# The first pass of a fused attention and gated FFN kernel: one program order on all five queues, the low weight bits cut out on ScalarE, and no float32 copies of two weight matrices

## The chip, the core and the metric

The kernel runs on one core of a Trainium2 chip. The metric is the device time of one execution in microseconds. The engines are named as the profile names them: PE (matrix multiply, with its weight loads as PEld), DVE (VectorE), ACT (ScalarE), POOL (GpSimd) and SP (the queue that issues the DMAs). Each engine works through its own queue strictly in order, and an instruction that waits holds up all that stand behind it on that queue.

## What is computed

Eight batches with eight heads of 576 queries and keys of width 64 go through an attention whose keys and values are first averaged in groups of eight, so that there are 72 of them. The result, 4608 rows of 512, goes through a gated feed-forward layer. The three weight matrices come in float64.

```python
k_p = k.reshape(B, H, Sp, pool, D).mean(axis=3)        # pool = 8, Sp = 72; v likewise
attn = softmax(q @ k_p.T / 8)
x = (attn @ v_p) as 4608 x 512
gate = 1 / (1 + exp(-(x @ w_gate)))                    # 512 x 1536
out = (gate * (x @ w_val)) @ w_out                     # 1536 x 512
```

## The kernel before, in words

**Blocks and passes.** The 4608 rows are cut into 12 blocks of 384 (`BT`). Six passes take two blocks each (side 0 and side 1). A pass has two halves: the chains, which make gate and value for 12 column groups `f` of 128 (kind G and V), and the second product, which sums over the 12 groups into six PSUM banks. Every float32 operand is split into a high and a low half of type fp32r, and a product is the three matmuls high·high, high·low, low·high. A chain of the first two passes (`whole`, L517) is thus 12 matmuls of 128x384, and one step of the second product (`second`, L615) is 18 matmuls of 128x512. From the third pass on a scheme with seven instead of eight products is used; the change doesn't touch it.

**Attention.** For a block `j` and a pair of heads `p` the steps are: sum keys in groups of eight on DVE, scale them into a block-diagonal tile on ACT (`kbd`), scores on PE (`sc`), maximum on DVE, exponentials on ACT, their total on DVE, division on POOL (`pm`), transposes on PE (`tp`), a high half on ACT and a low half on DVE, the product with the values on PE (`av`), and a copy into `xs`. The eight keys beyond 64 go a way of their own (`rest`, `r3`, `vres`). When both pairs of a half are there, `xs` is split into `xo`, the operand of the chains. Blocks 2 and 3, which the second pass needs, are computed during the first pass, blocks 4 and 5 during the second, and so on.

**Conversion.** `converted` (L155) takes a quarter-matrix tile of 128x1024 float64 words. `to_f32` (L112) makes float32 of it in five steps: an ACT instruction on the high words (L116), then on DVE a minimum (L118), a shift (L120), the sign (L122) and the three top bits of the low words (L126). Two ACT copies (L164) and two DVE subtractions (L166) make the halves. 12 such tiles make up the first two matrices. All halves go to DRAM (`keep`), and the float32 tile itself goes there too (`keptw`, L171). In the second pass `sums` (L178) loads that tile again and makes sums of quarters for the later passes (L182 to L184, L97, L98). The third matrix is converted in 12 tiles of 128x512 (`convert_o`, L211) beside the first pass's second product.

**What sets the order.** In the first pass the part `first_blocks` (L797) is written out by hand: blocks 0 and 1, tiles 0 and 1 of both matrices and the first eight chains stand in one list, and PE, DVE, ACT and POOL run it in that order. SP's queue there, and everything after this part (`hidden_first`, L541, then `second`), is put in order by a scheduler, which works from its own estimates. Key and value loads of the later blocks go through four buffers (`rawp`). The values of blocks 0 and 1 are pooled by matmuls in float32 (L926, L936), those of later blocks by DVE sums (L273).

Of the kernel before, what the change touches and what calls it, by code (L numbers as in the profile page):

```python
# [12 lines left out]
F32R = mybir.dt.float32r  # L13
U32 = mybir.dt.uint32
# [4 lines left out]
P = 128  # L19
B, H, S, D = 8, 8, 576, 64  # L20
POOL = 8
# [33 lines left out]
PLACE = {"k0": (0, 0), "k1": (0, 576), "k2": (0, 1152), "k3": (0, 1728), "R0": (0, 2304),  # L55
         "q0": (1, 0), "q1": (1, 384), "q2": (1, 768), "q3": (1, 1152), "V0": (1, 1536), "V1": (1, 2048), "V2": (1, 2560),
         "V3": (2, 0), "U0": (2, 512)}
# [3 lines left out]
def attention_then_ffn(ctx: ExitStack, tc: tile.TileContext, qT, kT, vm, vr, vn, sums8, wgv, wo, const, out, outT):  # L61
# [11 lines left out]
    cst = cpool.tile([P, P + 4], F32, name="cst")  # L73
    nc.sync.dma_start(cst, const)
    ident, mask = cst[:, :P], cst[:, P:]
# [30 lines left out]
    kept_w = {(kind, p): dram.tile([P, 4, HALF], F32, name=f"keptw{kind}{p}") for p in range(NP) for kind in "GVO"}  # L106
# [3 lines left out]
    words, parts, plain, oparts = {}, {}, {}, {}  # L110

    def to_f32(w, lo, hi):  # L112

        u = w.bitcast(U32)

        pinned(nc.scalar.activation(w, hi.bitcast(F32), AF.Abs, scale=2.0 ** -112))  # L116
        yield
        nc.vector.tensor_scalar(out=w, in0=w, scalar1=F64_MAX, scalar2=None, op0=ALU.min)  # L118
        yield
        nc.vector.tensor_scalar(out=u, in0=u, scalar1=3, scalar2=None, op0=ALU.logical_shift_left)  # L120
        yield
        nc.vector.scalar_tensor_tensor(  # L122
            out=u, in0=hi, scalar=0x80000000, in1=u, op0=ALU.bitwise_and, op1=ALU.bitwise_or
        )
        yield
        nc.vector.scalar_tensor_tensor(  # L126
            out=u, in0=lo, scalar=29, in1=u, op0=ALU.logical_shift_right, op1=ALU.bitwise_or
        )
        yield

    def fetch(kind, p):
        raw = big.tile([P, 4 * HALF, 2], U32, name="raw64", tag="big")
        nc.sync.dma_start(raw.rearrange("p n t -> p (n t)"), wgv[p, "GV".index(kind)].bitcast(U32))
        words[kind, p] = raw
# [11 lines left out]
    made = [0]  # L146

    def room_for_parts():

        made[0] += 1  # L150
        if made[0] <= 4 * NP and made[0] % 11 in (8, 9, 10):
            return work.tile([P, 2, 2, HALF], F32R, name="parts_x", tag=f"xo{(3, 6, 7)[made[0] % 11 - 8]}")
        return wpool.tile([P, 2, 2, HALF], F32R, name="parts", tag="parts")

    def converted(kind, p):  # L155
# [4 lines left out]
        w = (big if p else wpool).tile([P, 4, HALF], F32, name="w4", tag="big" if p else "parts")  # L160
        yield from to_f32(w.rearrange("p a n -> p (a n)"), raw[:, :, 0], raw[:, :, 1])
# [940 lines left out]
```

## Time and profile before

| | before |
|---|---|
| median of 3 runs | 1011.4 us (1011.3 to 1013.82) |
| the profiled execution | 1011.91 us |
| its span, first to last instruction | 1010.1 us |
| PE busy | 966.0 us (96%) |
| DVE busy | 674.4 us (67%) |
| ACT busy | 518.1 us (51%) |
| DMA | 267.08 MB, mean 264 GB/s |

The views give microseconds from the start of the span. A line such as `L122 DVE SCALAR_TENSOR_TENSOR w<-raw,w 128x1024 ... x12 | 14.6, 1216 | 0.2` reads: line 122 of the kernel, on DVE, 12 instructions that write `w` from `raw` and `w`, busy 14.6 us in all, 1216 ns each on average, and 0.2 us in which DVE stood idle just before them. A float32 matmul leaves two records; an fp32r matmul leaves one. The records of matmuls that run back to back overlap, so the pace of a dense stretch is read from the start of a group to the start of the next. In a table of stages the numbers behind each engine are its busy time and its records; PEclk is the granted clock of TensorE, 1.00 for full speed.

### The profile page before, as it was taken

What the parts mean: (1) busy time and instruction counts of PE and PEld (TensorE: products, weight loads), DVE (VectorE), ACT (ScalarE), POOL (GpSimd) and SP (SyncE); (2) the same over time, 40 slices, a digit from 0 to 9 for tenths busy, and PEclk for the clock granted to TensorE, in tenths of its full rate; (3) what the DMA queues carried; (4) which work ended last, traced back from release to release, by engine and by line L of the source; (5) the groups of instructions that cost most, each with busy time, mean ns of one, the idle gap of its engine ahead of it and who ended that gap; (6) DMA issues with size and microseconds to landing.
All of it is one profiled execution on the core that took longest, in us unless ns stands there. A gap on an engine that the chain in (4) does not pass through costs nothing.

```text
span 1010.1 us, 15339 instructions
## 1 busy us (share of the span) xinstructions
PE 966.0 (96%) x5448; PEld 918.1 (91%) x5448; DVE 674.4 (67%) x1149; ACT 518.1 (51%) x1034; POOL 47.4 (5%) x67
## 2 busy tenths in 40 slices
PE   5779999989999999999989999999999999999998
PEld 4569999768999988889979999998999999999998
DVE  5858898795666635675877666769566659244474
ACT  4647676554344432564645455656365546233342
POOL 2010000000000000000000000000000000000000
PEclk9979999999999999999999999999999999999999
DMA  9736999887999633899986877877877678867556
GB/s 335 247 119 223 337 368 361 272 274 279 344 322 337 223 132 116 307 376 362 320 289 196 288 258 239 267 261 249 288 270 222 217 247 250 289 233 247 195 188 229
DMA packets 117739, 267.08 MB, mean 264 GB/s; under 512 B 12448, under 2 KB 44448, under 8 KB 116128
## 3 DMA queue, kind: packets, MB, share of 16 engines
q1 hardware_dynamic: 117664, 266.12, 77.7%
q8 instruction: 43, 0.70, 0.3%
q14 instruction: 32, 0.26, 0.1%
HBM read 209.44 MB, written 56.62 MB: 263 GB/s over the span
## 4 chain that ended last, share of the span: by engine, by line
PE 79%; DVE 8%; DMA 7%; ACT 4%; issue 2%; SPq 0%; ACTq 0%; DVEq 0%
PE chain L486 30%; PE chain L526 16%; PE acc L725 15%; PE acc L634 8%; PE sc L330 3%; PE av L339 3%; DMA w<-keptwO 1%; PE tp L418 1%; DVE s L660 1%; PE vp L926 1%; DMA raw_o<-in_wo 1%; DVE hs L690 1%; DMA parts<-keptG1C 1%; DMA out<-o 1%; DMA w<-keptwG 1%
## 5 line engine op out<-in xcount | busy, mean ns | idle before, releaser
L486 PE MATMUL chain<-xo,parts 128*128 128x384 f32 x2016 | 375.7, 340 | 4.7 <-DMA parts<-keptV1A 1.1
L486 PEld LDWEIGHTS chain<-xo,parts 128*128 128x128 f32 x2016 | 349.2, 188 | 9.8 <-ACT sG L492 1.7
L526 PE MATMUL chain<-xo,parts 128*128 128x384 f32 x1008 | 188.2, 341 | 3.4 <-ACT parts L164 3.2
L725 PE MATMUL acc<-hs,oparts 128*128 128x384 f32 x1008 | 184.4, 338 | 2.4 <-DMA oparts<-keptS 1.0
L526 PEld LDWEIGHTS chain<-xo,parts 128*128 128x128 f32 x1008 | 175.7, 189 | 5.4 <-ACT parts L164 3.8
L725 PEld LDWEIGHTS acc<-hs,oparts 128*128 128x128 f32 x1008 | 175.8, 189 | 5.1 <-DVE hs L690 2.2
L634 PE MATMUL acc<-oparts,hs 128*128 128x512 f32 x432 | 104.4, 395 | 4.3 <-ACT hs L626 4.1
L634 PEld LDWEIGHTS acc<-oparts,hs 128*128 128x128 f32 x432 | 79.7, 188 | 21.8 <-ACT hs L626 5.2
L498 DVE TENSOR_TENSOR y<-chain,sG 128x384 f32<-128x384 f32 x72 | 39.6, 553 | 73.1 <-DMA out<-o 26.3
L412 POOL TENSOR_TENSOR pm<-e,rz 128x384 f32<-128x384 f32 x40 | 36.3, 907 | 700.5 <-DVE rz L393 415.0
L498 DVE TENSOR_TENSOR y<-chain,sV 128x384 f32<-128x384 f32 x72 | 39.4, 551 | 41.3 <-PE chain L486 30.2
L504 ACT ACTIVATE gate<-y 128x384 f32<-128x384 f32 x72 | 37.7, 525 | 37.8 <-DVE y L498 37.4
L492 ACT COPY sV<-chain 128x384 f32<-128x384 f32 x72 | 34.2, 475 | 44.3 <-PE chain L486 43.0
L690 DVE TENSOR_TENSOR hs<-h,hs 128x768 fp32r<-128x768 f32 x48 | 46.1, 965 | 15.5 <-ACT hs L689 15.5
L492 ACT COPY sG<-chain 128x384 f32<-128x384 f32 x72 | 34.3, 476 | 41.5 <-PE chain L486 41.3
L689 ACT CAST hs<-h 128x768 fp32r<-128x768 f32 x48 | 40.1, 835 | 24.0 <-PE acc L725 23.0
L689 ACT CAST hs<-s 128x768 fp32r<-128x768 f32 x36 | 29.6, 835 | 31.6 <-PE acc L725 21.5
L330 PE MATMUL sc<-kbd,raw 128*128 128x144 f32 (+1 forms) x256 | 42.5, 297 | 0.0
L507 DVE TENSOR_TENSOR h<-y,gate 128x384 f32<-128x384 f32 x72 | 39.7, 555 | 1.7
L330 PEld LDWEIGHTS sc<-kbd,raw 128*128 128x128 f32 (+1 forms) x256 | 33.6, 177 | 7.4 <-issue 4.5
L690 DVE TENSOR_TENSOR hs<-s,hs 128x768 fp32r<-128x768 f32 x36 | 34.3, 959 | 7.3 <-ACT hs L689 7.0
L422 DVE TENSOR_TENSOR pl<-tp,ph 128x384 fp32r<-128x384 f32 x40 | 22.0, 551 | 21.9 <-ACT ph L421 21.9
(159 smaller groups left out, 1177.1 us busy)
## 6 DMA issues: line engine op xcount, KB each, us to landing
oparts<-keptS SPq DMA_DIRECT2D x48, 512.0 KB, 5.0
oparts<-keptO SPq DMA_DIRECT2D x72, 256.0 KB, 3.7
raw<-in_wgv SPq DMA_DIRECT2D x12, 1024.0 KB, 7.7
raw<-in_qT SPq DMA_DIRECT2D x42, 192.0 KB, 4.3
raw<-in_kT SPq DMA_DIRECT2D x28, 288.0 KB, 5.5
raw<-in_vm SPq DMA_DIRECT2D x24, 256.0 KB, 4.6
raw_o<-in_wo SPq DMA_DIRECT2D x12, 512.0 KB, 5.5
keptO<-oparts SPq DMA_DIRECT2D x12, 512.0 KB, 4.2
```

The lines of the kernel that those rows point to most:

```text
L330: nc.tensor.matmul(sc[lo - i * P:hi - i * P, i], lhsT=q[:, lo:hi], rhs=kbd[slot(b, p)], start=True, stop=True)
L412: nc.gpsimd.tensor_tensor(out=pm, in0=e[:, n, :, :KM], in1=rz[:, n, :, None].broadcast_to([P, 2 * QT, KM]), op=ALU.mult)
L486: nc.tensor.matmul(t, lhsT=w[:, h, a], rhs=x[:, y, c], start=(m in (1, 2, 5) and c == 0 and k == 0), stop=(c == 1 and k == 2), skip_group_ ...
L492: nc.scalar.copy(s, t)
L498: nc.vector.tensor_tensor(out=y, in0=t, in1=seen[kind, {2: 1, 3: 6, 7: 5}[m]], op=ALU.add)
L504: nc.scalar.activation(gates[q[0]][:, q[1]], y, AF.Sigmoid)
L507: nc.vector.tensor_tensor(out=hb[f // 4][:, f % 4, q[0] * BT:(q[0] + 1) * BT], in0=y, in1=gates[q[0]][:, q[1]], op=ALU.mult)
L526: nc.tensor.matmul(t, lhsT=w[:, c // 2, h, a], rhs=x[:, y, c % 2], start=(c == 0 and k == 0), stop=(c == NC - 1 and k == 2),)
L634: nc.tensor.matmul(acc[i], lhsT=hs[:, y, a], rhs=o[:, w], start=(f == 0 and k == 0), stop=(f == NF - 1 and k == 2),)
L689: nc.scalar.copy(hs[:, 0], x)
L690: nc.vector.tensor_tensor(out=hs[:, 1], in0=x, in1=hs[:, 0].bitcast(F32), op=ALU.subtract)
L725: nc.tensor.matmul(acc[name, c], lhsT=w[:, k, h, c * P:(c + 1) * P], rhs=hs[:, y, k], start=(m in (1, 2, 5) and q == 0 and k == 0 and t == ...
```

## The change

**One order.** `first_blocks` and `hidden_first` are gone, and so is the scheduled first `second`. `first_pass` runs a table of some 900 words, from left to right, for all of the first pass: attention of blocks 0 to 3, all 24 conversions, all 48 chains, the second product and the stores. SP's loads and stores are in the table too. The loads named in `FIRST` stand ahead of the table; the second to fourth weight tile are no longer among them. An entry like `G.0.3@6` is the gate chain of block 0, group 3, in PSUM bank b4; `lr`, `lv`, `lk`, `lq` are loads; `rsum`, `vsum`, `keys` are sums on DVE.

**Values of block 1.** They are pooled on DVE from `in_vr` and `in_vm` like those of later blocks; only batch 0 is still pooled by matmuls.

**Low bits.** `to_f32` has the three low bits made by an ACT instruction (a scaled Relu on a 16-bit half of the low word), and the DVE shift is folded into the last of DVE's steps. DVE has three steps then instead of four, ACT two instead of one.

**No float32 copies.** `keptw` for the first two matrices is neither stored nor loaded. In the second pass `base` adds the two halves again: two DVE instructions of 128x512 per tile.

```diff
-FIRST = "k0 q0 k1 q1 k2 q2 k3 q3 U0 W0 V0 V1 V2 V3 R0 W1 W2 W3".split()
+FIRST = "k0 q0 k1 q1 k2 q2 k3 q3 U0 W0 V0 V1 V2 V3 R0".split()
+ORDER = """
+lr.1.1 rsum.1.1 rhi.1.1 lv.1.0 vsum.1.0 vhi.1.0 rlo.1.1 keys.0.0 put.0.0 lr.1.0 sc.0.0@0 rsum.1.0 rhi.1.0 rlo.1.0
+vput.1.0 lk.1.0 keys.1.0 vlo.1.0 put.1.0 lv.1.1 vsum.1.1 keys.0.1 lq.1.0 put.0.1 sc.1.0@1 lk.1.1 max.0.0 keys.1.1
...
-    def to_f32(w, lo, hi):
+    def to_f32(w, raw):
         u = w.bitcast(U32)
+        words = raw.rearrange("p (n t) -> p n t", t=2)
+        lo, hi = words[:, :, 0], words[:, :, 1]
         pinned(nc.scalar.activation(w, hi.bitcast(F32), AF.Abs, scale=2.0 ** -112))
         yield
+        half = raw.bitcast(U16).rearrange("p (n t) -> p n t", t=4)[:, :, 1]
+        nc.scalar.activation(lo, half, AF.Relu, scale=2.0 ** -13, bias=third)
+        yield
         nc.vector.tensor_scalar(out=w, in0=w, scalar1=F64_MAX, scalar2=None, op0=ALU.min)
         yield
-        nc.vector.tensor_scalar(out=u, in0=u, scalar1=3, scalar2=None, op0=ALU.logical_shift_left)
-        yield
-        nc.vector.scalar_tensor_tensor(
-            out=u, in0=hi, scalar=0x80000000, in1=u, op0=ALU.bitwise_and, op1=ALU.bitwise_or
-        )
-        yield
-        nc.vector.scalar_tensor_tensor(
-            out=u, in0=lo, scalar=29, in1=u, op0=ALU.logical_shift_right, op1=ALU.bitwise_or
-        )
+        nc.vector.scalar_tensor_tensor(out=lo, in0=hi, scalar=0x80000000, in1=lo, op0=ALU.bitwise_and, op1=ALU.bitwise_or)
+        yield
+        nc.vector.scalar_tensor_tensor(out=u, in0=u, scalar=3, in1=lo, op0=ALU.logical_shift_left, op1=ALU.bitwise_or)
         yield
...
-            if i:
-                nc.sync.dma_start(kept_w[kind, p], w)
...
+    def base(kind, p):
+        w = bases[kind, p] = big.tile([P, 8, HALF], F32, name="w8", tag="big")
...
+        for i, at in enumerate((slice(0, 4, 3), slice(1, 3))):
+            t = plain[kind, 2 * p + i].bitcast(F32)
+            nc.vector.tensor_tensor(out=w[:, at], in0=t[:, :, 0], in1=t[:, :, 1], op=ALU.add)
...
+        engines = (nc.vector, nc.scalar, nc.tensor, nc.gpsimd, nc.sync)
+        with tc.manual_schedule(engines={e.engine for e in engines}):
+            for word in ORDER.split():
+                what, _, named = word.partition("@")
...
+                does[what](*map(int, args))
```

The order that the change makes, at three places. First the start of DVE's queue. Before (`in_kT` has landed in `h`, the sums go to `early`, L869 is the maximum, L880 the total):

```order
L77 CAST identr_89<-cst_87 128x128
L855 TENSOR_REDUCE early_217<-h_220 128x72 x2
L869 TENSOR_REDUCE m_258<-sc_253 128x6
L855 TENSOR_REDUCE early_217<-h_220 128x72
L869 TENSOR_REDUCE m_273<-sc_262 128x6
L855 TENSOR_REDUCE early_217<-h_220 128x72
L869 TENSOR_REDUCE m_288<-sc_277 128x6
L880 TENSOR_REDUCE zs_302<-e_243 128x12
```

And now, with L360 the value sums (`raw_240` holds `in_vr`, `raw_246` holds `in_vm`), L1024 and L1011 low halves, L904 the key sums and L918 the maximum:

```order
L141 CAST identr_89<-cst_87 128x128
L360 TENSOR_REDUCE small_211<-raw_240 96x64
L360 TENSOR_REDUCE small_211<-raw_246 128x64
L1024 TENSOR_TENSOR otherV5_234<-small_211,otherV5_234 32x64
L904 TENSOR_REDUCE early_205<-h_208 128x72
L360 TENSOR_REDUCE small_211<-raw_255 96x64
L1024 TENSOR_TENSOR otherV5_234<-small_211,otherV5_234 32x64
L904 TENSOR_REDUCE early_205<-raw_268 128x72
L1011 TENSOR_TENSOR vl4_105<-small_211,vh4_100 64x64 x2
L360 TENSOR_REDUCE small_211<-raw_275 128x64
L904 TENSOR_REDUCE early_205<-h_208 128x72
L918 TENSOR_REDUCE early_205<-sc_259 128x6
```

Three instructions that belong to block 1's values stand ahead of the first key sum of block 0.

Second, SP's queue from the tenth load on. Before, the values (`in_vn`) are followed by three weight tiles (`in_wgv`):

```order
L816 DMA early_217<-in_sums8 128x360
L133 DMA raw64_230<-in_wgv 128x2048
L816 DMA early_216<-in_vn 128x512 x3
L816 DMA early_217<-in_vn 128x512
L816 DMA h_220<-in_vn 64x512
L133 DMA raw64_237<-in_wgv 128x2048
L133 DMA raw64_239<-in_wgv 128x2048
L133 DMA raw64_241<-in_wgv 128x2048
```

And now the loads that DVE's first two sums read, `raw_240` and `raw_246`, come right behind the whole of `FIRST`:

```order
L842 DMA early_205<-in_sums8 128x360
L198 DMA raw64_221<-in_wgv 128x2048
L842 DMA early_204<-in_vn 128x512 x3
L842 DMA early_205<-in_vn 128x512
L842 DMA xs1_210<-in_vn 64x512
L351 DMA raw_240<-in_vr 32x512 x3
L347 DMA raw_246<-in_vm 128x512
L351 DMA raw_255<-in_vr 32x512 x3
L340 DMA raw_268<-in_kT 128x576
```

The load that the first key sum needs is still SP's second; the loads that DVE waits for ahead of it are the 17th to 20th.

Third, PE where the chains begin. Before, four products of block 0 stand ahead of the first chain, and block 1's scores come behind it (L339 `av`, L526 chains, L330 scores):

```order
L339 MATMUL av_422<-early4_218,vh3_99 128x384 x2
L339 MATMUL av_422<-early4_218,vl3_104 128x384
L339 MATMUL av_422<-early4_219,vres3_109 128x384
L526 MATMUL chain_469<-xo1_431,parts_434 128x384 x6
L526 MATMUL chain_469<-xo2_460,parts_434 128x384 x6
L526 MATMUL chain_488<-xo1_431,parts_463 128x384 x6
L526 MATMUL chain_488<-xo2_460,parts_463 128x384 x6
L526 MATMUL chain_509<-xo1_431,parts_502 128x384 x6
L526 MATMUL chain_509<-xo2_460,parts_502 128x384 x6
L330 MATMUL sc_522<-kbd0_91,raw_444 128x144
```

Now block 1's scores, half of its `av` (L426) and most scores of blocks 2 and 3 (L417) stand ahead of it (L606 chains, L955 and L948 transposes):

```order
L417 MATMUL sc_690<-kbd2_93,raw_564 128x144 x3
L426 MATMUL av_700<-early4_207,vh1_97 128x192 x2
L426 MATMUL av_700<-early4_207,vl1_102 128x192
L426 MATMUL av_700<-pr_235,vres1_107 128x192
L426 MATMUL av_700<-early4_207,vh0_96 128x192 x2
L426 MATMUL av_700<-early4_207,vl0_101 128x192
L426 MATMUL av_700<-pr_235,vres0_106 128x192
L955 MATMUL tr_711<-identr_89,r3_634 96x128 x3
L948 MATMUL tp_716<-cst_87,pm1_230 128x128 x3
L606 MATMUL chain_732<-xo1_654,parts_625 128x384 x6
L606 MATMUL chain_732<-xo2_694,parts_625 128x384 x6
```

In PE's queue 64 score matmuls stand ahead of the second pass's first chain before, and 52 now: 12 of block 4's, and one set of three transposes, have moved into the second pass. The six ACT_TABLE_LOADs that ACT's queue still has in the first pass stand ahead of the first value sum's copy and at five changes between Exp and Sigmoid.

More of the change, by code (lines that the diff above doesn't have):

```diff
@@ L1029, in first_blocks, with step_o, product_g, product_v @@
[L1029 to L1035 removed]
+            next(conv[kind, p])
+        def step_o(f):
+            if f not in conv:
+                conv[f] = converted_o(f)
+            next(conv[f])
+        def product_g(j, f):
+            vbank["G", j, f] = whole("G", f, j, tags.pop(0))
+        def product_v(j, f):
+            vbank["V", j, f] = whole("V", f, j, tags.pop(0))
@@ new lines, in hs_lo, with accumulate @@
+        def hs_lo(f):
+            nc.vector.tensor_tensor(
+                out=hss[f][:, 1], in0=hb[f // 4][:, f % 4], in1=hss[f][:, 0].bitcast(F32), op=ALU.subtract
+            )
+        def accumulate(f, half):
+            for i in range(QT * half, QT * half + QT):
+                if f == 0:
+                    acc[i] = bank_for([P, DM], "acc")
+                a = slice(i * P, (i + 1) * P)
+                for k, (y, w) in enumerate(((0, 0), (1, 0), (0, 1))):
+                    nc.tensor.matmul(
+                        acc[i], lhsT=hss[f][:, y, a], rhs=oparts[f][:, w], start=(f == 0 and k == 0),
+                        stop=(f == NF - 1 and k == 2),
+                    )
```

542 lines of the change are left out of this document (295 added, 247 removed), and 4 rows, old and new, of the table banks.

## The prediction

> **What bounds the kernel now.** First the table of stages, cut at the first dense chains, the end of the conversions, the second pass's first chain and its last.
>
> ```profile
> core 0: us, PE busy (x) PEld busy (x) DVE busy (x) ACT busy (x) POOL busy (x), PEclk, DMA share, GB/s
> 0.00:85.00 85.00, 61.89 (x302) 51.55 (x303) 55.65 (x101) 47.13 (x127) 11.14 (x27) 0.88 0.65 229
> 85.00:175.00 90.00, 90.00 (x534) 89.76 (x533) 80.62 (x136) 63.61 (x138) 4.45 (x5) 1.00 0.95 338
> 175.00:241.00 66.00, 61.31 (x292) 48.69 (x290) 51.19 (x93) 34.94 (x73) 4.19 (x4) 1.00 0.79 265
> 241.00:354.00 113.00, 112.16 (x676) 111.26 (x674) 69.06 (x118) 49.71 (x86) 4.88 (x5) 1.00 0.89 308
> ```
>
> PE is the bound from 85 us on; the second pass leaves it idle for 0.84 us of 113. The loss is in the first 85 us, where PE is busy 61.89 and its granted clock is 0.88, and a little in 175:241. So the change can win only in the first pass. Then the timeline, for when work begins there.
>
> ```profile
> 4.26 0.75 DVE L855 TENSOR_REDUCE early<-h 128x72 f32<-128x576 f32 x1 [1.21 <-DMA h<-in_kT]
> ...
> 7.03 3.22 PE L330 MATMUL sc<-kbd,early 128*128 128x144 f32 x12 [7.03 <-ACT kbd L860]
> ...
> 31.93 6.28 PE L526 MATMUL chain<-xo,parts 128*128 128x384 f32 x24 [1.79 <-ACT parts L164]
> ...
> 240.96 17.04 PE L526 MATMUL chain<-xo,parts 128*128 128x384 f32 x96
> 257.84 0.49 PE L418 MATMUL tp<-cst,pm 128*128 128x128 f32 x3
> 258.08 4.24 PE L526 MATMUL chain<-xo,parts 128*128 128x384 f32 x23
> ```
>
> DVE starts at 4.26, PE at 7.03, the chains at 31.93, and the second pass at 240.96. 96 chain matmuls take 257.84 - 240.96 = 16.88 us, so 0.176 us is one at full clock, and three transposes are 0.24. The 24 chain matmuls at 31.93 would be 4.2 us at that pace and took 6.28: 2.1 lost to the clock.
>
> **The start.** DVE's first real instruction now waits for `in_vr`, which stands behind all of `FIRST`.
>
> ```profile
> 0.00:10.00 10.00, 2.97 (x12) 2.90 (x12) 3.15 (x5) 2.84 (x8) 2.45 (x19) 1.00 0.78 256
> 10.00:20.00 10.00, 6.64 (x28) 5.18 (x27) 7.93 (x18) 7.88 (x31) 2.50 (x3) 0.92 1.02 380
> ...
> 9.68 3.65 SPq L133 DMA_DIRECT2D raw<-in_wgv  x3
> ...
> SPq L133 <- DMA raw<-in_wgv: 2.1, 1, 2.1
> ```
>
> `FIRST` without the three weight tiles is four key loads of 295 KB, four query loads of 197 KB, the sums' matrix (184 KB), one weight tile (1049 KB) and 1.18 MB of values, with `const` 4.4 MB. At 256 and then 380 GB/s they are through at about 15 us. The queue shows the same: the third issue of the group at 9.68 waited 2.1 us for the weight tile issued eight places earlier, until about 13 us; the third piece of `in_vr` now stands in that place. I take it as landed at 15 to 15.5. Behind it come the sum, ACT's table load (1.28, quoted below), a copy and a low half, so the first key sum starts at about 17.0 instead of 4.26. Queued behind that wait are all of DVE, and through its sums ACT and PE.
>
> **From there to the first chain.** DVE's queue holds, from the first key sum to the last `xo` of block 0:
>
> ```profile
> L869 DVE TENSOR_REDUCE m<-sc 128x6 f32<-128x432 f32 x8 | 4.8, 597 | 5.6 <-PE sc L330 3.9 <-ACT kbd L860 1.7
> 13.77 1.04 DVE L880 TENSOR_REDUCE zs<-e 128x12 f32<-128x864 f32 x1
> ...
> 15.20 0.55 DVE L869 TENSOR_REDUCE m<-sc 128x6 f32<-128x432 f32 x1
> ...
> 19.91 0.85 DVE L120 TENSOR_SCALAR w<-w 128x1024 uint32<-128x1024 uint32 x1
> 20.69 0.54 DVE L915 TENSOR_TENSOR early<-tp,early 128x384 fp32r<-128x384 f32 x1
> ...
> L915 DVE TENSOR_TENSOR early<-tp,early 128x384 fp32r<-128x384 f32 x6 | 3.3, 553 | 4.5 <-ACT early L912 4.5
> L118 DVE TENSOR_SCALAR w<-w 128x1024 f32<-128x1024 f32 x12 | 8.2, 682 | 3.9 <-ACT w L116 3.8
> L120 DVE TENSOR_SCALAR w<-w 128x1024 uint32<-128x1024 uint32 x12 | 8.4, 700 | 0.1
> L120 DVE TENSOR_SCALAR raw_o<-raw_o 128x512 uint32<-128x512 uint32 x12 | 5.0, 420 | 0.1
> L122 DVE SCALAR_TENSOR_TENSOR w<-raw,w 128x1024 uint32<-128x1024 uint32 x12 | 14.6, 1216 | 0.2
> L126 DVE SCALAR_TENSOR_TENSOR w<-raw,w 128x1024 uint32<-128x1024 uint32 x12 | 15.2, 1263 | 0.1
> L961 DVE TENSOR_TENSOR vl<-vp,vh 128x128 fp32r<-128x128 f32 x4 | 1.2, 289 | 1.9 <-ACT vh L955 1.8
> L98 DVE TENSOR_TENSOR xo<-xs,xo 128x768 fp32r<-128x768 f32 x8 | 7.6, 955 | 2.8 <-ACT xo L97 2.8
> ```
>
> 18 key and value sums at the 0.75 of the key sum at 4.26 are 13.5; 12 maxima at 0.597, 7.2; 5 totals at 15.20 - 13.77 = 1.43, 7.2; 7 low halves at 0.553, 3.9; two conversions at 0.682 + 1.216 + 1.263, 6.3; 25 short ones at up to 0.289, 7.2; one part of 512 elements about 0.7 (the 0.692 of L182's additions, quoted below); two `xo` 1.9. That is 47.9 us, so the chains begin at 17.0 + 47.9 = 64.9, if what neighbouring records overlap pays for the waits inside (L120's record of 0.85 at 19.91 ends at 20.76, and the next begins at 20.69). PE has only some 22 us to do in that time and can't be the limit; ACT's longest pieces there are ten sets of exponentials. The chains thus start 33.0 us later than now.
>
> **After it PE has everything in one piece.** What is left of the first pass for PE from there:
>
> ```profile
> 360.98 5.02 PE L634 MATMUL acc<-oparts,hs 128*128 128x512 f32 x21
> 365.84 0.49 PE L418 MATMUL tp<-cst,pm 128*128 128x128 f32 x3
> ...
> 92.31 0.90 PE L330 MATMUL sc<-kbd,raw 128*128 128x144 f32 x6
> 92.95 2.34 PE L526 MATMUL chain<-xo,parts 128*128 128x384 f32 x12
> ```
>
> 576 chain matmuls at 0.1758 are 101.3; 216 of the second product at (365.84 - 360.98)/21 = 0.231, 50.0; 32 `av` at the chain's pace, 5.6, and 16 of half its width at about 0.11 (an estimate), 1.8; 11 sets of transposes at 0.24, 2.6; six score matmuls of two records each at 0.64/6 a record, 1.3. Together 162.6. One cold start as at 31.93 adds 2.1. Without another wait the first pass ends at 64.9 + 162.6 + 2.1 = 229.6.
>
> Can DVE and ACT feed it? From the last `xo` of block 0 to what the second product's first step needs, DVE's new queue holds ten whole conversions at 3.16 (31.6), five of the third matrix at half that length (about 1.8 each, 9.2), 23 parts or low halves of 512 at 0.70 (16.1), 17 halves of `h` at 0.55 (9.4), nine value sums at 0.75 (6.7), seven low halves at 0.553 (3.9), three totals at 1.43 (4.3), four maxima at 0.597 (2.4), two `xo` (1.9), four `oparts` at about 0.7 (2.8), and 28 short ones at 0.2 to 0.29 (about 7): 95 us, where the third matrix's, `h` and `oparts` are estimates from the quoted rows by size. PE arrives there 96 us after its first chain. Less the overlap, some 0.08 us at each of 80 to 90 places if 19.91 is typical, it is about 88 us of work in 96, a share of 0.92; the stage 85:175 had 80.62/90 = 0.90. So there is no room: if DVE can be busy for a share s, the wait is 88/s - 96, 2 us at 0.90 and 7.5 at 0.85. I take 4. End: 233.6.
>
> The folded shift is in these sums: it takes 12 x 0.700 + 12 x 0.420 = 13.4 us from DVE. ACT pays for it.
>
> ```profile
> L116 ACT ACTIVATE w<-raw 128x1024 f32<-128x1024 f32 x12 | 13.7, 1146 | 4.2 <-DMA raw<-in_wgv 4.1
> L116 ACT ACTIVATE raw_o<-raw_o 128x512 f32<-128x512 f32 x12 | 8.0, 670 | 9.9 <-DMA raw_o<-in_wo 8.9 <-PE acc L634 0.9
> L389 ACT ACT_TABLE_LOAD x6 | 7.7, 1283 | 1.1 <-DVE m L377 1.0
> L534 ACT ACT_TABLE_LOAD x5 | 6.4, 1283 | 0.1
> 43.59 1.28 ACT L983 ACT_TABLE_LOAD   x1
> 44.88 0.87 ACT L983 ACTIVATE y<-chain 128x384 f32<-128x384 f32 x2
> L182 DVE TENSOR_TENSOR w<-w 128x512 f32<-128x512 f32 x12 | 8.3, 692 | 13.5 <-DMA w<-keptwG 6.0 <-DMA w<-keptwV 5.9 <-DMA keptG4C<-sums 1.7
> ```
>
> 12 x 1.146 + 12 x 0.670 = 21.8 us more. The grouping of Exp and Sigmoid takes away at least five of the 11 table loads in the two rows, 6.4 us, so ACT, busy 145.7 of 241 now, rises to about 161: it has room on average. The row shows the whole price of a load: the next ACTIVATE starts at 44.88, right at its end.
>
> The Trainium skill, "ScalarE: Activation LUTs", section "What ACT_TABLE_LOAD costs", adds a drain of about 1.38 us to the 1.283. By it five loads would save 13.3 us, ACT would rise to 154, and the sum would stay as it is.
>
> **Work moved and copies dropped.** 12 score matmuls (2.6 us) and one set of transposes (0.2) move to the second pass, where PE has no gap, so they are paid there: +2.8. The stores and loads of `keptw` (12 x 512 KB each way) were hidden: PE was full at DMA shares of 0.95 and 0.89. In their place the second pass gets 24 additions at 0.692 = 16.6 us on a DVE busy 69.06 of 113. They lie beside the chains. Bounds: 0.8 won (all of PE's gap there) to 16.6 lost; I take +1, since DVE stays idle for over a fifth of the time.
>
> **Sum.** 233.6 + 2.8 + 1 = 237.4 against 240.96: 3.6 less. The profiled execution took 1011.9 us with a span of 1010.1, so 1008.3 by this account, and the median of 1011.4 becomes 1007.8. A difference under 0.3% (3 us) can't be told from none here.
>
> **Rivals.**
>
> 1. The forecast: late start, dense after it. 0.42. It spreads from 1003 to 1013 by the landing at 15 (give or take 1.5) and the wait of 0 to 7.5.
> 2. No loss but the start: DVE's records overlap throughout (47.9 falls to about 44), no wait, no cold start, nothing lost in the second pass. Then 61 + 162.6 + 2.8 = 226.4, 14.6 less: 997. For it: 85:175 and 241:354 run without a gap. Against: DVE idles 29 of the first 85 us now. 0.25.
> 3. Slower: PE starves in the conversion stage. DVE, ACT and PE wait for each other in strict order, and DVE's share s decides: at 0.85 the wait is 7.5, 3.5 more than taken, and from there down the change stops paying; at 0.78, between 0.655 (0:85) and 0.90 (85:175), it is 17 us: 1007.8 + 13 = 1020.8. Each gap also costs clock.
>
> ```profile
> 50.00:60.00 10.00, 10.00 (x43) 7.60 (x43) 6.40 (x13) 5.91 (x20) 2.29 (x2) 0.70 0.63 222
> ```
>
> PE was busy throughout here, after gaps, at a granted 0.70. The Trainium skill, "TensorE: Matmul & The Clock Gate", section "What's actually happening", has the clock halve after an idle window of about 3.4 us and return after as much busy time. The gap before 31.93 was 1.79 us and the 24 matmuls behind it were still slow, so by this trace shorter gaps can be followed by a slow stretch. 0.25.
> 4. The second pass becomes tight: additions and moved work delay the gates, 5 us instead of 1: 1011.8, no difference. 0.08.
>
> That the order isn't what the table says is no rival: it stands so in each queue.
>
> **Chances.** Faster by over 0.3% (under 1008.4): 0.25 and 0.28 of the first, 0.53. Within: 0.12 of the first and the 0.08, with 0.03 of the third, 0.23. Slower (over 1014.4): 0.02 and 0.22, 0.24. The range from 997 to 1019 leaves out half of the third and the far end of the second.
>
> **What would show it.** Right: the first DVE sum at 15 to 16 us, PE's first score at 18 to 19, its first chain at 62 to 68, the clock at 1.00 from 70 on, and the second pass beginning around 232. Wrong: `in_vr` landing before 12 us; PE waiting for `parts` or `hs` over 8 us between 70 and 230; the second pass longer than 120 us.

## The result and the profile after

The changed kernel took 1020.1 us (median of five runs, 1019.9 to 1024.4), the kernel before beside it 1011.4 us (five runs, 1010.0 to 1014.0). The ratio is 1.0091, with an interval of 1.0064 to 1.0118: it is slower by 0.9%, where 1007.8 was forecast, in a range up to 1019. The profiled execution took 1020.1 us with a span of 1018.4, which is 8.3 more than before.

First the stages, in the same cuts as before the change.

```profile
0.00:85.00 85.00, 53.55 (x279) 44.79 (x279) 62.44 (x113) 53.83 (x167) 15.32 (x31) 0.90 0.76 248
85.00:175.00 90.00, 86.96 (x488) 83.17 (x489) 80.90 (x139) 72.22 (x148) 3.94 (x4) 1.00 0.86 288
175.00:241.00 66.00, 62.84 (x304) 55.22 (x303) 29.05 (x43) 24.88 (x40) 0.00 (x0) 0.97 0.56 190
241.00:354.00 113.00, 113.00 (x674) 110.19 (x673) 84.37 (x152) 50.84 (x90) 6.34 (x6) 1.00 0.78 262
```

PE has 53.55 us of work in the first 85 instead of 61.89, and now also waits between 85 and 175 (86.96 of 90, where it was full). ACT does 53.83 and 72.22 instead of 47.13 and 63.61. The second pass is full. Next the timeline at the places that the prediction named: DVE's first sums, PE's first scores, the first chain, PE's longest wait behind it, and the place where the second pass begins.

```profile
18.05 1.40 DVE L360 TENSOR_REDUCE small<-raw 96x64 f32<-96x512 f32 x2 [14.98 <-DMA raw<-in_vr]
...
19.71 0.75 DVE L904 TENSOR_REDUCE early<-h 128x72 f32<-128x576 f32 x1
...
21.13 1.78 PE L417 MATMUL sc<-kbd,early 128*128 128x144 f32 x6 [21.13 <-ACT kbd L909]
...
68.19 6.63 PE L606 MATMUL chain<-xo,parts 128*128 128x384 f32 x36 [0.22 <-ACT early L969]
...
191.67 0.52 PE L948 MATMUL tp<-cst,pm 128*128 128x128 f32 x3 [3.16 <-ACT xs L1038]
191.95 5.97 PE L1094 MATMUL acc<-oparts,hs 128*128 128x512 f32 x18
...
226.32 2.09 PE L606 MATMUL chain<-xo,parts 128*128 128x384 f32 x11
...
245.47 2.10 PE L606 MATMUL chain<-xo,parts 128*128 128x384 f32 x11
```

DVE does wait for `in_vr`, as forecast, and 14.98 us long. The chains begin at 68.19. The rows at 226.32 are already the second pass's: 16 of its chain matmuls, 2.8 us, run ahead of the last product of the first pass, so that the first pass's own work ends at about 245.47 - 2.8 = 242.7. The third pass begins at 412.18 (before: 406.95).

| | forecast | measured | later by |
|---|---|---|---|
| first key sum | 17.0 | 19.71 | 2.7 |
| first chain | 64.9 | 68.19 | 3.3 |
| end of the first pass's work | 233.6 | 242.7 | 9.1 |
| third pass begins | 403.35 (406.95 less 3.6) | 412.18 | 8.8 |
| span | 1006.5 (1010.1 less 3.6) | 1018.4 | 11.9 |

So 3.3 us are missing at the start, 5.8 between the first chain and the end of the first pass, and 3.1 after the second pass, while the second pass itself costs 0.3 less than taken.

### The profile page after: what moved, and what is told of

The parts are those of the page before. It is cut to its first block, busy times and chain, and to the rows that moved or that the text cites. A ratio compares the mean times of both kernels' runs of the same rounds, so it can differ in the third digit from the quotient of the medians.

```text
span 1018.4 us, 15269 instructions
## 1 busy us (share of the span) xinstructions
PE 963.3 (95%) x5424; PEld 917.4 (90%) x5424; DVE 679.9 (67%) x1154; ACT 528.2 (52%) x1061; POOL 48.4 (5%) x67
## 4 chain that ended last, share of the span: by engine, by line
PE 74%; DMA 10%; DVE 9%; ACT 4%; issue 2%; SPq 0%; DVEq 0%; ACTq 0%
PE chain L566 30%; PE acc L787 15%; PE chain L606 14%; PE acc L696 5%; PE acc L1094 4%; PE sc L417 3%; PE av L426 3%; DMA w<-keptw 1%; DMA raw_o<-in_wo 1%; DMA out<-o 1%; PE tp L505 1%; DMA parts<-keptG3B 1%; DMA h<-in_kT 1%; DMA parts<-keptG1C 1%; DVE s L722 1%
## 5 line engine op out<-in xcount | busy, mean ns | idle before, releaser
L606 PE MATMUL chain<-xo,parts 128*128 128x384 f32 x1008 | 186.3, 340 | 2.6 <-DVE h L1075 2.2
L606 PEld LDWEIGHTS chain<-xo,parts 128*128 128x128 f32 x1008 | 175.1, 188 | 5.5 <-DVE h L1075 2.8
L499 POOL TENSOR_TENSOR pm<-e,rz 128x384 f32<-128x384 f32 x32 | 29.1, 910 | 624.6 <-DVE rz L479 410.9
L417 PE MATMUL sc<-kbd,raw 128*128 128x144 f32 (+1 forms) x280 | 49.8, 311 | 4.4 <-ACT e L923 2.3
L417 PEld LDWEIGHTS sc<-kbd,raw 128*128 128x128 f32 (+1 forms) x280 | 38.7, 187 | 12.8 <-issue 6.3
```

The source lines that it names most:

```text
L417: nc.tensor.matmul(sc[lo - i * P:hi - i * P, i], lhsT=q[:, lo:hi], rhs=kbd[slot(b, p)], start=True, stop=True)
L606: nc.tensor.matmul(t, lhsT=w[:, c // 2, h, a], rhs=x[:, y, c % 2], start=(c == 0 and k == 0), stop=(c == NC - 1 and k == 2),)
```

## The experiments

The theory at this point (S): the loss is the late start, and whatever moves the first chain moves the end by as much. Its rivals: (C) DVE and ACT set the pace of the conversions, so that an earlier start only makes PE wait later; (L) at the start it isn't DVE's order but the loads that hold everything. The runs, with the places of the timeline in their profiled executions; a ratio is that to the kernel before, timed on the same chip. That kernel's own median was 1011.4 us beside the changed kernel and 1012.2 to 1013.7 beside the others, so medians of runs that were not timed together can differ by some 2 us for that alone, and the ratios are the better comparison:

| run | first chain | second pass | third pass | span | median | ratio |
|---|---|---|---|---|---|---|
| before | 31.93 | 240.96 | 406.95 | 1010.1 | 1011.4 | |
| changed | 68.19 | 245.47 | 412.18 | 1018.4 | 1020.1 | 1.0091 (1.0064 to 1.0118) |
| a1 | 66.85 | 244.40 | 411.11 | 1017.3 | 1019.2 | 1.0066 (1.0043 to 1.0089) |
| a2 | 68.25 | 247.44 | 414.14 | 1019.4 | 1021.2 | 1.0082 (1.0057 to 1.0108) |
| a3 | 69.76 | 248.25 | 414.95 | 1021.4 | 1022.8 | 1.0096 (1.0071 to 1.0121) |
| a4 | 68.67 | 255.33 | 422.10 | 1026.0 | 1030.5 | 1.0178 (1.0149 to 1.0207) |
| a5 | 76.22 | 255.57 | 422.52 | 1027.6 | 1028.4 | 1.0143 (1.0122 to 1.0164) |
| a6 | 64.62 | 240.20 | 406.91 | 1012.3 | 1016.1 | 1.0030 (1.0012 to 1.0048) |
| a7 | 69.48 | 244.25 | 410.96 | 1014.9 | 1020.9 | 1.0080 (1.0054 to 1.0107) |
| a8 | 70.74 | 247.21 | 413.92 | 1020.0 | 1017.2 | 1.0045 (1.0024 to 1.0065) |
| a9 | 69.13 | 242.78 | 409.49 | 1015.7 | 1017.0 | 1.0044 (1.0025 to 1.0064) |
| a10 | 69.93 | 246.99 | 413.69 | 1019.3 | 1021.4 | 1.0086 (1.0064 to 1.0108) |
| a11 | 68.40 | 242.50 | 409.20 | 1015.7 | 1017.8 | 1.0045 (1.0029 to 1.0061) |
| a12 | 59.66 | 232.65 | 399.35 | 1004.9 | 1006.6 | 0.9932 (0.9910 to 0.9954) |
| b1 | 31.35 | 235.01 | 406.04 | 1010.2 | 1012.3 | 0.9995 (0.9978 to 1.0011) |
| b2 | 32.34 | 239.28 | 414.44 | 1015.9 | 1019.9 | 1.0067 (1.0048 to 1.0085) |

Single executions of one kernel spread over 1.6 us (a12) to 8.2 us (a9), so a profiled execution may lie beside its median: a8's is the slowest of its ten runs, a7's is the fastest of its six. A difference of 1 to 3 us between two profiles is therefore only an indication.

### The start: what is passed on

**a5, ten more sums**, a cost added at the suspected place:

```diff
-lr.1.1 rsum.1.1 rhi.1.1 lv.1.0
+lr.1.1 rsum.1.1 extra.10 rhi.1.1 lv.1.0
+        def extra(n):
+            for _ in range(n):
+                pool(vs[3], cst[:, :D, None].broadcast_to([P, D, POOL]), nc.vector)
```

> Ten more value sums of the constant tile (0.68 to 0.70 us each, 7 us in all, into a place that is written again later) stand in DVE's queue right behind the first value sum, ahead of block 0's first key sum. Theory S (the start is passed on whole): first chain 7 us later, at 75, second pass and end 7 us later, about 1027. Rival C (the dense stretch absorbs it): first chain at 75, second pass's first chain 0 to 3 us later, 1020 to 1023. Rival L (until some 40 us the loads set the pace, not DVE): first chain 0 to 3 us later, end as much.

The ten sums are one row of DVE's timeline, and the first chain answers it.

```profile
18.74 7.16 DVE L359 TENSOR_REDUCE small<-cst 128x64 f32<-128x512 f32 x10
...
76.22 6.84 PE L605 MATMUL chain<-xo,parts 128*128 128x384 f32 x36
```

7.16 us more on DVE put the first chain 8.0 us later, the second pass 10.1, the median 8.2 (5.3 by the ratios, 1.0143 against 1.0091). S holds for a delay: nothing behind the first chain takes it up. That an earlier first chain is passed on too, against C, this run can't show; a6 and a12 below do.

**a1, block 0 first**: some twenty words of the table are moved to its beginning, the loads stay.

```diff
+keys.0.0 put.0.0 sc.0.0@0 keys.0.1 put.0.1 max.0.0 exp.0.0 sc.0.1@2 keys.0.2 max.0.1 exp.0.1 put.0.2 keys.0.3 put.0.3
+sum.0.0 rest.0.0 again.0.0 sc.0.2@2 main.0.0 max.0.2
 lr.1.1 rsum.1.1 rhi.1.1 lv.1.0 vsum.1.0 vhi.1.0 rlo.1.1
```

> Block 0's four key sums, three maxima, one total and one set of remainder parts are put ahead of block 1's value sums in the table; all loads stay where they are. That is 4 x 0.74 + 3 x 0.60 + 1.45 + 0.75 = 7.0 us of DVE's work, which then lies in the 15 us in which DVE waits for in_vr. Theory S (the late start is passed on whole, since DVE is busy 46.86 of the 50.2 us from 18 to 68.2): first chain at 61 instead of 68.19, everything behind it 7 us earlier, about 1013. Rival C (from 68 on DVE and ACT set the pace of the conversions, so that an earlier first chain only makes PE wait longer there): first chain at 61 too, PE's waits from the first chain to 190 grow from 7 to 12 or more, end 0 to 3 us earlier, 1017 to 1020.

**a2, the weight tile and block 0's values later** (`first.N` issues the N-th load of `FIRST`):

```diff
-        for what in FIRST:
+        for what in FIRST[:8]:
-... sc.0.1@2 lv.3.0 max.0.1 exp.0.1 vsum.3.0 keys.0.2 lq.1.1 sc.1.1@0
+... sc.0.1@2 lv.3.0 max.0.1 exp.0.1 vsum.3.0 keys.0.2 lq.1.1 first.8 first.9 first.10 ... first.14 sc.1.1@0
```

> The order of the engines is as changed; on SP's queue the sums' matrix, the first weight tile and block 0's values (seven loads, 2.4 MB) are moved from ahead of block 1's first loads to behind the load lq.1.1, some fourteen loads further down. Theory S: in_vr lands at 9 to 10.5 us instead of 18, DVE's first sums are 7.5 us earlier, first chain at 61 and 1013, unless the moved values or the weight tile now come late for the value products (47 us) and the first conversion (42 us); then part of it is lost. Rival C: first chain at 61, end at most 3 us earlier. Rival L (all loads of the first 40 us are needed by the same time, so that their sum and not their order sets the pace): first chain no more than 2 us earlier.

Neither did what S expected: the first chain came 1.3 us earlier and not at all. PE's timelines show why, a1 first.

```profile
12.92 1.78 PE L416 MATMUL sc<-kbd,early 128*128 128x144 f32 x6 [2.55 <-ACT kbd L908]
22.78 2.31 PE L416 MATMUL sc<-kbd,raw 128*128 128x144 f32 x8 [8.09 <-DMA raw<-in_qT]
```

And a2:

```profile
14.64 1.78 PE L416 MATMUL sc<-kbd,early 128*128 128x144 f32 x6 [14.64 <-ACT kbd L911]
...
34.22 1.81 PE L416 MATMUL sc<-kbd,raw 128*128 128x144 f32 x6 [7.30 <-DMA raw<-in_qT]
```

PE's first scores begin at 7.15 us in a1 and at 14.64 in a2 instead of 21.13, but then PE waits for a query load that isn't there: in a1 8.09 us for block 1's first, which stood behind the weight tile and block 0's values; in a2 7.30 us for block 2's first, ahead of which these had now been put.

**a7, both together**, with the value sums where their loads should land and block 0's values (`first.8` and `first.10` to `first.14`) behind `lq.1.2`:

```diff
+lr.1.1 lv.1.0 lr.1.0 lk.1.0 keys.0.0 put.0.0 sc.0.0@0 keys.0.1 put.0.1 sc.0.1@2 keys.0.2 put.0.2 max.0.0 exp.0.0
+... rsum.1.1 rhi.1.1 lv.1.1 vsum.1.0 vhi.1.0 lq.1.0 rsum.1.0 rhi.1.0 lk.1.1 first.9 sum.0.0 main.0.0 ...
```

> Order and loads of the start together: block 1's first values and keys are loaded right behind block 0's keys and queries, the first weight tile behind six of them, block 0's values behind sixteen; in the table block 0's sums, maxima, first total and first exponentials come first, and each value sum stands where its load should have landed and frees its buffer for the next load. Theory S with L (DVE's 48.5 us up to the first chain are fixed, and what is gained is idle time of DVE before 34 us, of which a1 had some 13 us): first chain at 56 to 62, second pass and end 6 to 12 us earlier, 1008 to 1014. If the loads' sum alone sets the pace: first chain at 65 or later, 1016 to 1021.

The number of the second case came: 69.48. DVE had nothing to do for 6.11 us, until a key load of block 3 that now stood behind block 0's values.

```profile
30.57 0.68 DVE L359 TENSOR_REDUCE small<-raw 128x64 f32<-128x512 f32 x1
37.35 0.75 DVE L906 TENSOR_REDUCE small<-raw 128x72 f32<-128x576 f32 x1 [6.11 <-DMA raw<-in_kT]
```

**a6, no value loads**: the value sums of the first pass read the constant tile.

```diff
-            pool(vs[p], raws["v", j, p], nc.vector)
+            pool(vs[p], cst[:, :D, None].broadcast_to([P, D, POOL]), nc.vector)
```

> Leaves out all loads of pooled values in the first pass (eight of 256 KB, twelve of 64 KB); the value sums read the constant tile instead, with as many elements, so the values of blocks 1 to 3 are not those of the reference. DVE has the same work and waits for no value. Theory S with L (the loads ahead and their buffers set the pace of the first 40 us): DVE starts at 4.4 and the first chain is at 53 to 60, the end as much earlier, 1006 to 1013. If DVE's own 48.5 us alone set it, first chain at 53. Rival C: first chain earlier by as much, PE's waits behind it grow and the end is at most 3 us earlier, 1017 or more.

With these loads gone the first chain is 3.6 us earlier and the second pass 5.3, so an earlier start is passed on as well; PE still waits 10.39 us for the first query of block 1 (18.22), which now stands behind block 0's loads, the weight tile and one key load. L it is: loads hold the start. Open was whether it is the four load buffers with the queue's order, or the transfers as such.

**a10, more buffers; a11, the same with a8's edit** (below):

```diff
     def load(*what):
+        if early_loads[0]:
+            early_loads[0] -= 1
+            return fill(wpool.tile([P, S], F32, name="raw", tag="parts"), *what)
         return fill(rawp.tile([P, S], F32, name="raw"), *what)
+lr.1.1 lv.1.0 lr.1.0 lk.1.0 lv.1.1 lq.1.0 lk.1.1 lk.3.0 keys.0.0 put.0.0 sc.0.0@0 ...
+... lk.3.1 first.9 first.8 first.10 first.11 first.12 first.13 first.14 ...
```

> The table of a1 (block 0's first steps ahead); the first eight loads of values, keys and queries behind block 0's get a place of their own (the tiles of the first two matrices' parts, empty until 57 us), so that four more can be under way before one of the four load buffers has to be read; the first weight tile and block 0's values are loaded behind them, before 30 us. If buffers and order of the loads set the time of DVE's work up to 35 us (theory L): PE waits for in_qT under 3 us instead of 12, block 3's second key sum at 27 to 30 instead of 34 to 37, first chain at 60 to 63, second pass and end as much earlier, 1012 to 1015. If the transfers themselves are the bound (6 to 8 MB at some 300 GB/s until 25 us): key sum at 33 or later, first chain at 66 or later, 1017 or more.

> The same with a8's copy ahead. If both losses are on the path one behind the other: 2 to 4 us less than a10, 1009 to 1013, near the kernel before. If a8's 3 us came from elsewhere: as a10.

**a12, loads in the order of their use**: twelve early places instead of eight, and the weight tile and block 0's values behind `lq.2.2`, that is, behind block 1's last keys:

```diff
-... lk.3.1 first.9 first.8 first.10 first.11 first.12 first.13 first.14 ... lk.1.2 ... lk.1.3 lq.2.2
+... lk.3.1 ... lk.1.2 ... lk.1.3 lq.2.2 first.9 first.8 first.10 first.11 first.12 first.13 first.14
```

> As a11, with four more places for the first loads (twelve in all), and the first weight tile and block 0's values loaded behind block 1's last keys instead of ahead of them (in a10 DVE waited 6.97 us for those keys, in_kT, at 39.05). If each load's place in the queue against the time of its use sets the start (theory L): DVE's wait of 7 us goes, first chain at 60 to 64, end 4 to 8 us before a11's, 1010 to 1014, even with the kernel before or ahead of it. If the transfers together are the bound: the wait turns up at the weight tile or at block 0's values, first chain at 66 or later, within 2 us of a11's 1017.8.

DVE in a10: block 3's second key sum is at 31.32 instead of 35.61, and then the gain is lost again at block 1's keys.

```profile
31.32 0.75 DVE L911 TENSOR_REDUCE small<-raw 128x72 f32<-128x576 f32 x1 [3.08 <-DMA raw<-in_kT]
39.05 0.76 DVE L911 TENSOR_REDUCE early<-h 128x72 f32<-128x576 f32 x1 [6.97 <-DMA h<-in_kT]
```

The same two sums in a12, without a wait, and the first chain there.

```profile
26.32 0.74 DVE L912 TENSOR_REDUCE small<-raw 128x72 f32<-128x576 f32 x1
26.98 0.74 DVE L912 TENSOR_REDUCE early<-h 128x72 f32<-128x576 f32 x1
...
59.66 6.62 PE L611 MATMUL chain<-xo,parts 128*128 128x384 f32 x36 [0.21 <-ACT early L977]
```

Against a11 the first chain is 8.7 us earlier, the second pass 9.9, the median 11.2; at 1006.6 the whole change with these loads and a8's copy is faster than the kernel before (0.9932, 0.9910 to 0.9954). C falls with it. So the sum of the transfers did not hold the start; the places of the loads, in the queue and in buffers, did. The two aren't separated: eight more buffers without the order of use gained nothing (a11's first chain is at 68.40, a1's at 66.85), and whether a12's order would have been enough with four buffers was not tried. The stages of 10 us show it on the DMA's side (last two columns: share and GB/s), the changed kernel first,

```profile
10.00:20.00 10.00, 0.00 (x0) 0.00 (x0) 1.87 (x4) 0.69 (x3) 0.00 (x0) 1.00 0.94 283
20.00:30.00 10.00, 7.18 (x32) 5.60 (x33) 9.27 (x18) 5.97 (x26) 0.00 (x0) 0.94 0.64 195
```

then a12:

```profile
10.00:20.00 10.00, 3.26 (x13) 2.00 (x12) 8.28 (x17) 4.95 (x21) 1.61 (x2) 0.68 0.84 248
20.00:30.00 10.00, 8.36 (x40) 6.77 (x41) 9.05 (x17) 6.04 (x25) 0.00 (x0) 0.63 1.03 374
```

DVE has 8.28 us of work from 10 to 20 instead of 1.87, and the DMA engines, at a share of 0.64 in 20:30 of the changed kernel, run full.

### The wait at 191.67

**a8, one copy ahead; a9, with a7's start.**

```diff
-... turn.3.2@6 ol.8 oconv.8 oconv.8 oconv.8 x.3.0 oconv.7 hi.3.2
+... turn.3.2@6 x.3.0 ol.8 oconv.8 oconv.8 oconv.8 oconv.7 hi.3.2
```

> One copy (x.3.0, block 3's product out of PSUM) is put ahead of the conversion of the ninth tile of the third matrix in ACT's queue, where it stood behind two steps that waited 4 us for the load of in_wo. If that wait is the cause of PE's 3.16 us at 191.67 and of the slow matmuls behind it (18 in 5.97 us, where others take 4.29): second pass 3 to 5 us earlier, 1015 to 1017. If the load and not the copy's place sets the pace of the second product there: the wait turns up at the next part of the third matrix, and the end moves less than 1 us.

> The two together. If both losses stand one behind the other on the path: the sum of the two gains, 9 to 17 us, 1003 to 1011. If the conversions' pace takes the place of the one removed: no more than the larger of the two.

ACT in the changed kernel: the copy that PE waits for (L1038) could run from 186.1, when the product that it copies ends, and stands behind two steps of a conversion whose load came at 189.86.

```profile
185.42 0.48 ACT L1070 ACTIVATE y<-chain 128x384 f32<-128x384 f32 x1
189.86 0.66 ACT L183 ACTIVATE raw_o<-raw_o 128x512 f32<-128x512 f32 x1 [3.96 <-issue]
190.43 0.75 ACT L187 ACTIVATE raw_o<-raw_o,cst 128x512 uint32<-128x512 uint16 x1
191.07 0.46 ACT L1038 COPY xs<-av 128x384 f32<-128x384 f32 x1
```

In a8 PE does not wait there, and the product behind it has its normal pace again.

```profile
193.01 0.82 PE L947 MATMUL tp<-cst,pm 128*128 128x128 f32 x6
193.58 4.38 PE L1093 MATMUL acc<-oparts,hs 128*128 128x512 f32 x18
199.38 2.35 PE L605 MATMUL chain<-xo,parts_x 128*128 128x384 f32 x12 [1.42 <-DVE otherG L963]
```

3.16 of waiting and 5.97 - 4.38 = 1.6 of slow matmuls go, and 1.42 come back at 199.38: 3.3 us. The median is 2.9 lower than the changed kernel's (4.7 by the ratios, whose intervals touch), as expected; in the profiled execution another wait, 1.95 at 126.19, takes part of it. Two more pairs have the same edit: a9 is 3.9 below a7, and a11 3.6 below a10. a9 is no better than a8, since a7 had gained nothing that it could add.

### The conversion

**a3, DVE's shift back**: `to_f32` as before the change, inside the new order. **b1**: ACT's low bits in the kernel before, everything else as it was.

```diff
-        nc.scalar.activation(lo, half, AF.Relu, scale=2.0 ** -13, bias=third)
+        nc.vector.tensor_scalar(out=u, in0=u, scalar1=3, scalar2=None, op0=ALU.logical_shift_left)
```

> The conversion as before the change inside the new order: DVE shifts and combines in three steps and ACT makes no low bits. DVE gets 12 x 0.70 + 12 x 0.42 = 13.4 us more in the first pass, ACT about 12 x 1.22 + 12 x 0.76 = 24 us less. If DVE has no room in the dense stretch (0.94 busy from 68 to 110, 0.90 from 110 to 150): PE's waits grow by most of the 8 us that fall into it, 1026 to 1030. If the pace is set by ACT (0.91 busy from 68 to 110) or by loads: no later, or a few us earlier, 1014 to 1020.

> The kernel before with one part of the change: ACT makes a weight's low bits, DVE's fourth step goes. DVE has 12 x 0.70 + 12 x 0.42 = 13.4 us less in the first pass, ACT 24 us more. If DVE held the conversions back before (PE idle 23 of the first 85 us): second pass 3 us or more earlier, 1008 or less. If not, since PE is busy throughout from 85 to 175: 1010 to 1013. If ACT becomes the bound (47 busy of the first 85): 1014 or more.

In a3 13.4 us more on DVE make the second pass 2.8 us later; by the ratios it can't be told from the changed kernel. DVE's room was larger than it looked, but ACT has 24 us less to do in a3, so the price of the shift by itself isn't shown. The stage from 110 to 150, the changed kernel's row and then a3's:

```profile
110.00:150.00 40.00, 38.01 (x218) 36.41 (x217) 36.05 (x58) 32.54 (x66) 1.87 (x2) 1.00 0.89 296
```

```profile
110.00:150.00 40.00, 35.94 (x207) 34.57 (x207) 39.35 (x63) 23.78 (x53) 1.86 (x2) 1.00 0.84 279
```

DVE can be busy 39.35 of 40 us, a share of 0.98, with PE losing two. In b1 the second pass begins 6 us earlier, but then takes 5 us longer, because the scheduler moves work across the border (PE has 169.22 us of work from there to the third pass instead of 165.15); nothing is left (0.9995).

### The copies

**a4, copies back** in the changed kernel; **b2, no copies** in the kernel before, with the additions:

```diff
+        if f % 2:
+            nc.sync.dma_start(kept_c[kind, f // 2], whole_w.pop((kind, f // 2)))
...
-            nc.vector.tensor_tensor(out=w[:, at], in0=t[:, :, 0], in1=t[:, :, 1], op=ALU.add)
+        nc.sync.dma_start(w[:, :4], kept_c[kind, p])
```

> The float32 copies of the first two matrices are stored and loaded again, and the 24 additions of the second pass are gone. If both are hidden, as forecast: the second pass from its first dense chain to its last stays within 1 us of the 113.6, the time within 2 us of 1020. If the additions delay the gates: second pass 1 us or more shorter. If the copies' 6.3 MB each way were in the way of other transfers (DMA share 0.82 to 0.89 from 110 to 190): conversions wait longer for in_wo, second pass begins 3 us or more later, 1023 or more.

> The kernel before with another part of the change: no float32 copies of the first two matrices are stored or loaded, the second pass adds the halves. If the 9.9 us of the run with the copies back come from the buffer that a copy's store holds in the new order (the weight's tile stands among the four tiles of the third matrix's parts, where it did not before): here the copies were hidden, 1010 to 1013. If they come from the transfers themselves (DMA share 0.95 from 85 to 175 before): first pass 3 us or more shorter, 1008 or less. If the additions cost: second pass 1 to 5 us longer. If leaving the copies out slows the later passes (603.2 us from the third pass on before, 606.2 after, PE's order being the same): 605 or more here too.

In a4 the second pass takes 369.01 - 255.33 = 113.7 us without the additions, as with them (113.6): they cost nothing. But it begins 9.9 us later. ACT's waits from 68 to 190 name the copies' stores; the changed kernel has no such rows.

```profile
ACT oparts L299 <- DMA keptwV<-w: 5.4, 2, 4.7
...
ACT oparts L299 <- DMA keptwG<-w: 2.1, 1, 2.1
...
ACT w L185 <- DMA keptwG<-w: 1.5, 1, 1.5
```

A weight's float32 tile is now one of the four tiles of `opool`, and a store holds it: 9.0 us in these rows. Not all of that reaches PE. Its waits between first chain and second pass are 13.7 us instead of 7.4, and the longest new one follows from a store:

```profile
152.27 0.62 ACT L299 CAST oparts<-raw_o 128x512 fp32r<-128x512 f32 x1 [4.74 <-DMA keptwV<-w]
...
155.42 3.76 PE L608 MATMUL chain<-xo,parts_x 128*128 128x384 f32 x12 [3.60 <-ACT y L1072]
```

ACT's sigmoid, for which PE waits here, stands behind the conversion that the store held. For the rest of the 9.9 us (2.40 at 124.54 behind DVE, 4.17 instead of 3.16 at a8's place, slower matmuls behind both) the store isn't shown as the cause; the transfers themselves, at a DMA share of 0.95 instead of 0.78 from 68 to 110, may have part in it. b2 shows no gain from dropping the copies where the tile stood in `big`; it is 0.7% slower, with a second pass of 122.2 instead of 113.0 us, in which PE has 119.54 us of work. The scheduler ordered that kernel anew from the first pass on, so how much of it the additions are stays open.

## Why the prediction was wrong

The direction was wrong, by a sum of which each part is small.

1. **The landing of `in_vr`.** The step that failed first: "I take it as landed at 15 to 15.5". The queue, the wait and who stands behind it were right. So were the issue of the third piece, at 12.8 us, and the count of the bytes: 4.5 MB had been moved by 15 us. The changed kernel's stage up to there, and the time of that piece from its issue to its landing:

```profile
0.00:15.00 15.00, 0.00 (x0) 0.00 (x0) 0.50 (x1) 1.28 (x1) 2.47 (x19) 1.00 0.88 300
DMA to landing us min/median/max: 5.2/5.2/5.2
```

The step took the passing of the bytes for the landing, which left the piece some 2.5 us behind its issue. It took 5.2, and the first sum began at 18.05. The profile before had the size of this: in its first 25 us no kind of load but the small `in_const` landed in less than 4.4 us (median). Why a piece of 64 KB takes 5.2 us isn't shown; from 14 us on the engines moved fewer bytes at a full share (last section). So the first key sum was 2.7 us late, and the first chain 3.3.

2. **DVE's 47.9 us up to the first chain** were 48.5. Right: DVE was busy 45.26 us of them, and the overlap of its records did pay for the waits. PE had 38.1 us of work there and not 22, and still wasn't the limit. That the first chain could not be moved by DVE's order alone (a1) was not seen: at the start, loads and not DVE's first instruction are the limit.
3. **162.6 + 2.1 + 4 = 168.7 us from there** were 242.7 - 68.2 = 174.5. PE's waits were 7.4 instead of 4. Up to 165 us they were 4.25, and DVE's share was 39.41/41.80 = 0.94 from 68 to 110 and 36.05/40 = 0.90 after, so what was said of DVE held in size. The other 3.16 is ACT's queue at 191.67, which no step of the prediction had (a8). Of the remaining 2.4 us, 1.6 are slow matmuls. The cold start put at the first chain came to 0.1 there (36 matmuls in 74.66 - 68.19 = 6.47 us, 6.33 by the pace of 0.1758). Instead the matmuls behind the wait at 191.67 cost 1.6, and those behind the smaller waits about 2, an estimate from the starts of the groups (behind 1.29 at 145.00, 24 matmuls take 4.69 instead of 4.22): 3.7 in place of 2.1. In a12, where no wait of PE in this stretch is over 1.59 us, the stretch takes 232.65 - 2.8 - 59.66 = 170.2.
4. **The folded shift** was taken as 13.4 us of room on a queue without room. a3 puts the shift, less what ACT pays for it, at 2.8 us or less. The model of waiting by busy share, 88/s - 96, is too steep, since DVE reached 0.98.
5. **Moved work and additions**, +3.8: the changed kernel lost 412.18 - 406.95 - (242.7 - 240.96) = 3.5 there, and a4 puts the additions' part at nothing. The sum was right, its split wasn't. That the copies were hidden holds for the old place of the tile at best; with them back in the new order the second pass begins 9.9 us later (a4).
6. **Behind the second pass** nothing was forecast, and 3.1 us were lost: from the third pass on 606.2 us instead of 603.2, with PE's matmuls in the same order but for two. The kernels made from the changed one have 603.9 to 606.5, b1 604.2, b2 601.5. These are single executions, and in most kernels those differ by 4 us and more, so it isn't shown that the change costs anything there. The cause stays open.

The rival on the slower side gave 1020.8, which is the time that came, but not its mechanism: it had PE starve in the conversions for 17 us. The wait there was as forecast. The range was too narrow since the misses of the landing (3), of the dense stretch (6) and of the later passes (3) all fell on one side, and the last two had no row of their own in it.

The clock: the row at 191.95 shows 18 matmuls in 5.97 us behind a gap of 3.16, and the granted clock was 0.71 from there to 197.76, with 0.51 from 194 to 196. The Trainium skill's rule ("TensorE: Matmul & The Clock Gate", "What's actually happening": half the clock after an idle window of about 3.4 us) agrees in the half, but not in the length of the gap: this one is shorter than the window, and the one of 1.79 in the trace before, with 0.51 from 32 to 34 us, is far shorter.

## What to carry to other kernels

When the order of the engines is fixed beforehand, look at the queue of loads against the time of first use before anything else: a delay at the start of a strict order is passed on whole (7.2 us of added work put the first chain 8.0 us later), and a load is late by what is queued ahead of it and by the buffer that it needs. Take its landing from the times from issue to landing in the trace, not from the bytes that stand ahead. Gaining at one place only moved the wait to the next load, three times; the run that gained the 9 us had more buffers and the order of use together. Where a tile is moved to another pool, a transfer that was hidden may now hold what others wait for.

## What the runs showed of the hardware

DVE's short instructions take longer while POOL multiplies. DVE in the changed kernel, with POOL at work from 30.26 to 31.88, and the same two lines later, with POOL idle:

```profile
30.44 0.73 DVE L438 CAST r<-rest 128x96 fp32r<-128x96 f32 x1
31.20 0.79 DVE L439 TENSOR_TENSOR r<-rest,r 128x96 fp32r<-128x96 f32 x1
...
62.32 0.23 DVE L438 CAST r<-rest 128x96 fp32r<-128x96 f32 x1
62.58 0.26 DVE L439 TENSOR_TENSOR r<-rest,r 128x96 fp32r<-128x96 f32 x1
```

0.73 and 0.79 us instead of 0.23 and 0.26: about 1 us for each such pair on a queue that was the bound. The Trainium skill has this as a lock on a shared pair of ports that the later instruction waits for ("SBUF — State Buffer", "Who interferes with whom"); the ends agree, 31.17 on DVE after POOL's first multiplication of 0.83 us ended at 31.09.

A full DMA share is not a fixed rate. In the changed kernel's start:

```profile
12.00:14.00 2.00, 0.00 (x0) 0.00 (x0) 0.00 (x0) 0.00 (x0) 0.00 (x0) 1.00 1.04 399
14.00:16.00 2.00, 0.00 (x0) 0.00 (x0) 0.00 (x0) 0.00 (x0) 0.00 (x0) 1.00 1.09 248
```

At a share of 1.04 the engines moved 399 GB/s, and 2 us later, at 1.09, 248. The length of the rows doesn't explain it: by the trace both stretches hold packets of 2 KB alone, but for some of 4 bytes, and one of 2 KB took 84 ns (median) in the first and 152 in the second. The loads are `in_vn` first, then `in_vr` and `in_vm`. What slowed the later ones stays open.
